# A two-bank tile for the first product of a state-exchange MoE kernel, with a new hand order for its first batch and a moved read in its last

## The chip, the cores and the metric

The kernel runs on one core of one Trainium2 chip. The metric is the device time of one execution in microseconds (us). Of the kernel before, three runs took 654.80, 655.16 and 655.46 us; their median, 655.16 us, is the time before. TensorE is called PE here, its weight loads PEld, VectorE DVE, ScalarE ACT, GpSimd POOL and SyncE SP, as in the profile.

## The reference

An attention between tokens and a small state, in both directions, feeds a two-layer feed-forward part with a piecewise quadratic in between:

```python
# x [8, 8, 512, 64], state [8, 8, 32, 64]  (batch, head, rows, 64)
scores = scale * x @ state.T            # softmax over 32 states
xread  = softmax(scores) @ state
scores2 = scale * state @ x.T           # softmax over 512 tokens
sread  = softmax(scores2) @ x
rows = concat([xread, sread], axis=2)   # -> [8 * 544, 512], heads side by side
h = rows @ w_in                         # [4352, 2048]
g = where(h >= 1, h, where(h <= -1, 0, (h + 1)**2 / 4))
out = g @ w_out                         # [4352, 512]
```

## The kernel before, in words

**Batches.** The eight batches of 512 token rows are worked one after the other, and the 256 `sread` rows of all batches together at the end as a ninth (`b == B`). For a token batch `xread @ w_in` is never formed from `xread`: the state is multiplied into `w_in` first (`sw`, a chunk of 256 columns at a time, one group of matmuls on 64x32 pieces of the array), and the normalised weights `ath`/`atl` are multiplied with that.

**Precision.** Each fp32 operand of a large product is split in two (`..h` a rounded high part, made by a copy on ACT; `..l` the rest, made by a subtraction on DVE), and each product is three matmuls: high x high, high x low, low x high (L473 to L475 for the first product, L529 to L531 for the second).

**A step.** Per batch there are eight steps `j`, each 256 columns wide. The first product (`product(0)` and `product(1)`, six matmuls each) goes to two PSUM tiles of one bank, tag `h`, two buffers. Then ACT takes `relu(0)`, `relu(1)` (L478) and `square` (L481), DVE `bound(0)`, `bound(1)` (L484, which reads the product in PSUM again), ACT `high` (L493, `gh`) and DVE `low` (L498, `gl`). The second product (`g2`, eight groups of three matmuls) of step `j` is issued after the first product of step `j + 1`, into four `acc` tiles of a bank each. PSUM has eight banks: four `acc`, two `h`, and one two-bank tile `mm` that scores, transposed weights and `sw` share. The tag `h` also holds `sr`, the read of the tokens by the state (`read2`, L323), in steps `j == 0` of later batches, and the two banks of the `sw` pair (chunks 5 and 6) in steps `j == 4`.

**Later batches** (L789 on) are written as a plain loop. The framework puts each engine's instructions in order from that program, by its own estimate of when each is ready, program order deciding between ready ones; a tile's buffer is given to the next user when all instructions that touch it are done. In the step `j == 0`, the loop issues the first product, the whole second product of the batch before, the `sr` read and its scaling (`scale2`, L331, DVE), four chunks of `sw` in two pairs that borrow the four `acc` banks, and, if there is a next batch, that batch's scores. After them come the splits of the chunks (L434 on ACT, L435 on DVE).

**The first batch** is different, since the weights have to be brought in: `w_in` and `w_out` arrive as eight chunks each of 1 MB in a wide format, and each takes two conversions (`high` L583 on ACT, `low` L575 on ACT or L570 on DVE), a join on DVE (L591) and, for `w_out`, a split (L598 on ACT, L602 on DVE). All of this is woven between the attention of batches 0 and 1 and the eight steps of batch 0. The weaving is a list, `ORDER` (L20): each word is the number of an operation and the engine that runs it (S, P, A, D). `Plan` (L37) computes begin times from the costs that the operations are given, sorts by them, emits in that order, and fills planned gaps of PE between the first scores and the first second product with `warm` matmuls (L170). Inside this stage the framework reorders nothing. `w_in` chunks are staged in two buffers (`raw`), so the DMA of each waits for the join of the chunk two before.

PE's order in the first batch of the kernel before (`p` is a first product half, with two numbers before the split by attention half; `g2.half.j`): warm, sc0, sw0, sw1, four half products of j=0, e2p0, p0(1), sw2, p1(1), g2.0.0, sr0, p0(2), sw3, p1(2), g2.1.0, sc1, p0(3), g2.0.1, p1(3), g2.0.2, sw4, g2.1.1, rt0, p0(4), sw5, p1(4), ... and a ninth `sw`, chunk 0 of batch 1, at the end.

Of the kernel before, what the change touches and what calls it, by code (L numbers as in the profile page):

```python
# [8 lines left out]
F32 = mybir.dt.float32  # L9
# [100 lines left out]
def state_exchange_moe(  # L110
# [42 lines left out]
    def ps_h(name):  # L153
        return ps.tile([P, 512], F32, tag="h", bufs=2, name=name)
# [42 lines left out]
    class Attention:  # L197
# [60 lines left out]
        def inv1(self, q):  # L258
            _, _, s = self.parts(q)
            nc.vector.tensor_scalar_add(s, s, 1e-9)  # L260
            nc.vector.reciprocal(out=s, in_=s)
# [113 lines left out]

    sw_of = {}

    def sw_product(b, c, n):

        pt = ps_mm(f"sw{b}_{c}")  # L380
        for i in range(n):
            for pr in range(NPR):
                for hh in range(2):
                    rows = slice(hh * 64, hh * 64 + 64)
                    nc.tensor.matmul(  # L385
                        pt[pr * NS:(pr + 1) * NS, hh, i * CI:(i + 1) * CI],
                        lhsT=sb[rows, b, pr], rhs=w32[c + i][rows, pr], start=True, stop=True,
                    )
        w = n * CI
        wh, wl = (  # L390
            v[:, :2 * w].rearrange("p (q f) -> p q f", q=2) for v in split_tiles(f"sw{b}_{c}")
        )
        sw_of[b, c] = pt[:, :, :w], wh, wl
        for i in range(n):
            cols = slice(i * CI, (i + 1) * CI)
            chunk[b, c + i] = wh[:, :, cols], wl[:, :, cols]

    def sw_high(b, c):
        pt, wh, _ = sw_of[b, c]
        nc.scalar.copy(out=wh, in_=pt)  # L400

    def sw_low(b, c):
        pt, wh, wl = sw_of[b, c]
        nc.vector.tensor_tensor(out=wl, in0=pt, in1=wh.bitcast(F32), op=ALU.subtract)

    def sw_make(b, c, n):
        sw_product(b, c, n)
        sw_high(b, c)
        sw_low(b, c)

    def sw_pair(pieces, banks, whole=None):
# [20 lines left out]
        def split():  # L432
            for h, lo, pt in parts:
                nc.scalar.copy(out=h, in_=pt)  # L434
                nc.vector.tensor_tensor(out=lo, in0=pt, in1=h.bitcast(F32), op=ALU.subtract)  # L435
# [13 lines left out]
    class Hidden:  # L449


        def __init__(self, b, j):
            self.b, self.j = b, j
            self.u = work.tile([P, 2, S], F32, tag="u", bufs=1, name=f"u{b}_{j}")
            self.hs = []

        def product(self, i, ks=None):
# [19 lines left out]
        def relu(self, i):  # L477
            nc.scalar.activation(out=self.u[:, i], in_=self.hs[i], func=AF.Relu, scale=0.5, bias=half)  # L478
# [4 lines left out]
        def bound(self, i):  # L483
            nc.vector.scalar_tensor_tensor(  # L484
                out=self.u[:, i], in0=self.u[:, i], scalar=1.0, in1=self.hs[i],
                op0=ALU.min, op1=ALU.max,
            )
# [118 lines left out]
    plan = Plan({"raw": 2, "mm": 1, "tmp": 2, "u": 1, "h": 2, "g": 2, "w": 2, "e2": 1, "xt": 1, "xn": 1})  # L606
# [278 lines left out]
```

## Time and profile before

| | |
|---|---|
| median of three runs | 655.16 us (654.80 to 655.46) |
| the profiled execution | 655.44 us, of which 653.6 us are its span |
| PE busy in the span | 643.5 us, 98% |
| ACT, DVE busy | 363.3 us (56%), 339.9 us (52%) |
| granted TensorE clock, mean | 0.999 |
| HBM traffic | 34.08 MB read, 8.91 MB written |

The span runs from the first to the last instruction; the rest of the time lies around it. A matmul's own duration includes its way through the array, so PE's rate is read from starts: matmuls of 512 columns follow each other every 0.227 us. Most of the run is the loop over batches 1 to 7, each 72.5 us long.

### The profile page before, as it was taken

The page shows a single profiled execution, that of the slowest core. Times are in us where ns is not written, and L with a number is a line of the kernel's source. Part 1 is how long each engine was busy: PE and PEld are TensorE (multiplying, and loading weights), DVE is VectorE, ACT ScalarE, POOL GpSimd, SP SyncE. Part 2 cuts the span into 40 slices and gives each one's busy share as a digit, 9 for nine tenths or more (in the row PEclk, how much of TensorE's full clock was granted, in tenths as well). Part 3 has the DMA queues.
Part 4 walks back from the last instruction along what each step waited for, and adds up shares of the span by engine and source line. Part 5 has one row for each costly group of instructions (what it writes and reads, how often), then busy time and mean ns, then how long its engine had stood idle before and what let it go on. Part 6 is the DMA issues. An engine that isn't in the chain of part 4 may idle for free.

```text
span 653.6 us, 10359 instructions
## 1 busy us (share of the span) xinstructions
PE 643.5 (98%) x4438; PEld 519.8 (80%) x4438; DVE 339.9 (52%) x511; ACT 363.3 (56%) x485; POOL 0.8 (0%) x7
## 2 busy tenths in 40 slices
PE   8899999999999999999999999999999999999997
PEld 6677787878787887878787887878787878788895
DVE  5998967533483338443574339343664335334431
ACT  4999856544565446554564456444664455444632
POOL 0000000000000000000000000000000000000000
PEclk9999999999999999999999999999999999999999
DMA  8996005000310004000500004000300010000101
GB/s 336 413 378 258 0 1 195 0 2 1 147 48 1 0 20 175 1 2 1 192 2 1 0 34 163 0 1 1 129 1 1 0 67 0 2 1 1 64 1 33
DMA packets 11085, 43.64 MB, mean 67 GB/s; under 512 B 1312, under 2 KB 1440, under 8 KB 7968
## 3 DMA queue, kind: packets, MB, share of 16 engines
q1 hardware_dynamic: 6096, 34.28, 13.4%
q10 hardware_dynamic: 4944, 8.72, 3.6%
q8 instruction: 34, 0.56, 0.3%
q14 instruction: 11, 0.09, 0.0%
HBM read 34.08 MB, written 8.91 MB: 66 GB/s over the span
## 4 chain that ended last, share of the span: by engine, by line
PE 96%; DVE 2%; ACT 0%; issue 0%; DMA 0%; POOL 0%; SPq 0%; POOLq 0%
PE acc L529 19%; PE acc L531 19%; PE acc L530 19%; PE h L473 10%; PE h L474 10%; PE h L475 10%; PE sw L421 4%; PE sr L323 1%; PE sc L225 1%; PE e2p L305 1%; PE warmed L170 1%; PE sw L385 1%; DVE w L591 1%; DMA out_dram<-o 0%; DVE z L232 0%
## 5 line engine op out<-in xcount | busy, mean ns | idle before, releaser
L529 PE MATMUL acc<-wo,gh 128*128 128x512 f32 x544 | 214.0, 393 | 0.0
L531 PE MATMUL acc<-wo,gl 128*128 128x512 f32 x544 | 211.9, 390 | 0.0
L530 PE MATMUL acc<-wo,gh 128*128 128x512 f32 x544 | 211.9, 390 | 0.0
L478 ACT ACTIVATE u<-h,half 128x512 f32<-128x512 f32 x136 | 93.1, 689 | 179.8 <-PE h L475 170.4
L484 DVE SCALAR_TENSOR_TENSOR u<-u,h 128x512 f32<-128x512 f32 x136 | 87.3, 682 | 196.5 <-ACT u L481 196.2
L529 PEld LDWEIGHTS acc<-wo,gh 128*128 128x128 f32 x544 | 102.1, 188 | 24.4 <-issue 3.3
L531 PEld LDWEIGHTS acc<-wo,gl 128*128 128x128 f32 x544 | 102.1, 188 | 21.7
L530 PEld LDWEIGHTS acc<-wo,gh 128*128 128x128 f32 x544 | 102.2, 188 | 20.5
L498 DVE TENSOR_TENSOR gl<-u,gh 128x1024 fp32r<-128x1024 f32 x68 | 83.3, 1225 | 58.1 <-ACT gh L493 58.1
L493 ACT CAST gh<-u 128x1024 fp32r<-128x1024 f32 x68 | 71.4, 1051 | 63.5 <-DVE u L484 63.5
L481 ACT ACTIVATE u<-u 128x1024 f32<-128x1024 f32 x68 | 72.1, 1061 | 1.8
L421 PE MATMUL sw<-w,sb 64*32 64x256 f32 x880 | 27.0, 379 | 0.0
L544 ACT COPY o<-acc 128x512 f32<-128x512 f32 x33 | 19.0, 583 | 12.1 <-PE acc L531 12.1
L473 PE MATMUL h<-ath,sw_1h 128*128 128x512 f32 x60 | 24.4, 407 | 0.9 <-DVE u L484 0.9
L474 PE MATMUL h<-ath,sw_1l 128*128 128x512 f32 x60 | 23.5, 392 | 0.2 <-DVE sw_1l L435 0.2
L473 PE MATMUL h<-ath,sw_5h 128*128 128x512 f32 x60 | 23.6, 393 | 0.0
L473 PE MATMUL h<-ath,sw_3h 128*128 128x512 f32 x60 | 23.5, 391 | 0.0
L474 PE MATMUL h<-ath,sw_5l 128*128 128x512 f32 x60 | 23.4, 390 | 0.0
L475 PE MATMUL h<-atl,sw_5h 128*128 128x512 f32 x60 | 23.4, 389 | 0.0
L475 PE MATMUL h<-atl,sw_1h 128*128 128x512 f32 x60 | 23.4, 389 | 0.0
L475 PE MATMUL h<-atl,sw_3h 128*128 128x512 f32 x60 | 23.4, 389 | 0.0
L474 PE MATMUL h<-ath,sw_3l 128*128 128x512 f32 x60 | 23.3, 389 | 0.0
(184 smaller groups left out, 733.2 us busy)
## 6 DMA issues: line engine op xcount, KB each, us to landing
xt<-in_xt_dram SPq DMA_DIRECT2D x16, 512.0 KB, 5.0
raw_i<-in_moe_w_in_dram SPq DMA_DIRECT2D x8, 1024.0 KB, 6.0
raw_o<-in_moe_w_out_dram SPq DMA_DIRECT2D x8, 1024.0 KB, 11.4
xn<-in_x_dram SPq DMA_DIRECT2D x8, 1024.0 KB, 6.0
out_dram<-o ACTq DMA_DIRECT2D x32, 256.0 KB, 2.0
sb<-in_state_dram SPq DMA_DIRECT2D x1, 448.0 KB, 12.8
out_dram<-o SPq DMA_DIRECT2D x4, 64.0 KB, 1.7
out_dram<-o ACTq DMA_DIRECT2D x4, 64.0 KB, 2.0
```

The lines of the kernel that those rows point to most:

```text
L421: nc.tensor.matmul(banks[hh][pr * NS:(pr + 1) * NS, cols], lhsT=sb[rows, b, pr], rhs=w32[c][rows, pr], start=True, stop=True,)
L473: nc.tensor.matmul(o, lhsT=wh[:, k, sl], rhs=ah[:, k], start=first, stop=False)
L474: nc.tensor.matmul(o, lhsT=wl[:, k, sl], rhs=ah[:, k], start=False, stop=False)
L475: nc.tensor.matmul(o, lhsT=wh[:, k, sl], rhs=al[:, k], start=False, stop=last)
L478: nc.scalar.activation(out=self.u[:, i], in_=self.hs[i], func=AF.Relu, scale=0.5, bias=half)
L481: nc.scalar.activation(out=self.u, in_=self.u, func=AF.Square)
L484: nc.vector.scalar_tensor_tensor(out=self.u[:, i], in0=self.u[:, i], scalar=1.0, in1=self.hs[i], op0=ALU.min, op1=ALU.max,)
L493: nc.scalar.copy(out=gh, in_=self.u)
L498: nc.vector.tensor_tensor(out=gl, in0=self.u, in1=gh.bitcast(F32), op=ALU.subtract)
L529: nc.tensor.matmul(a, lhsT=lh, rhs=oh, start=f == 0, stop=False)
L530: nc.tensor.matmul(a, lhsT=lh, rhs=ol, start=False, stop=False)
L531: nc.tensor.matmul(a, lhsT=ll, rhs=oh, start=False, stop=f == NF - 1)
```

## The change

Four things change together.

- **One tile for the first product.** The tag `h` becomes one buffer of two banks in place of two buffers of one. `product(i)` writes bank `i` of it. `sr` takes the whole tile (using a corner of bank 0), and the `sw` pair of step `j == 4` takes both its banks.
- **First batch, fewer and larger operations.** `relu` and `bound` run once over both banks (128x1024); the two `inv1` of an attention become one pair of small instructions over both halves (in the loop's `first` as well). The chunks of `sw` are made as (0), (1), (2), (3, 4), (5, 6), (7 and batch 1's 0): three alone and three pairs, where there were nine alone. The loop over later batches goes on calling `relu(i)` and `bound(i)` bank by bank.
- **First batch, another order.** `ORDER` is replaced, and some costs in the plan are other numbers. PE's order becomes: warm, sc0, sw0, two half products of j=0, sw1, the other two, sw2, p0(1), p1(1), e2p0, g2.0.0, sr0, p0(2), sw3+4, p1(2), g2.1.0, sc1, p0(3), g2.0.1, p1(3), g2.0.2, g2.1.1, p0(4), sw5+6, p1(4), g2.1.2, g2.0.3, p0(5), rt0, p1(5), sw7+, g2.1.3, p0(6), g2.0.4, p1(6), g2.1.4, g2.0.5, p0(7), e2p1, p1(7), g2.0.6, g2.1.5, g2.1.6. The DMA order on SP becomes xt0, i0, i1, o0, o2, i2, o1, i4, xn0, i3, sb, xt1, i6, o7, o3, o6, i5, o4, i7, o5, xn1 (`i` and `o` are chunks of `w_in` and `w_out`; before: o0, o1, i2, i3, xt1, o2, xn0, o3, sb, o4, i4, i5, o7, o5, xn1, i6, i7, o6). DVE's order up to the first second product is: turns and maxima of batch 0, less, sum, inv1, w0, norm, back, norm, swl0, atl, back, w1, atl, top2, low i2, swl1, w2, top2, bound(0), join o0, swl2, gl(0), wol 0.
- **Last batch (b = 7), step j == 0.** `read2` is issued behind the four `sw` chunks instead of ahead of them, and `scale2` behind their splits.

```diff
     def ps_h(name):
-        return ps.tile([P, 512], F32, tag="h", bufs=2, name=name)
+        return ps.tile([P, 2, 512], F32, tag="h", bufs=1, name=name)
...
-        def inv1(self, q):
-            _, _, s = self.parts(q)
-            nc.vector.tensor_scalar_add(s, s, 1e-9)
-            nc.vector.reciprocal(out=s, in_=s)
+        def inv1(self):
+            nc.vector.tensor_scalar_add(self.s1, self.s1, 1e-9)
+            nc.vector.reciprocal(out=self.s1, in_=self.s1)
...
-            sr = ps_h(f"sr{b}") if b else ps_mm(f"sr{b}")[:, 0]
+            sr = (ps_h if b else ps_mm)(f"sr{b}")[:, 0]
...
         def first(self):
-            for f in (self.top1, self.less1, self.exp1, self.sum1, self.inv1, self.norm1):
+            for f in (self.top1, self.less1, self.exp1, self.sum1):
                 for q in range(2):
                     f(q)
+            self.inv1()
+            for q in range(2):
+                self.norm1(q)
...
         def product(self, i, ks=None):
...
-            if not ks or 0 in ks:
-                self.hs.append(ps_h(f"h{b}_{j}_{i}"))
-            hp = self.hs[i]
+            if i == 0 and (not ks or 0 in ks):
+                self.h = ps_h(f"h{b}_{j}")
+            hp = self.h[:, i]
...
-        def relu(self, i):
-            nc.scalar.activation(out=self.u[:, i], in_=self.hs[i], func=AF.Relu, scale=0.5, bias=half)
+        def relu(self, i=slice(None)):
+            nc.scalar.activation(out=self.u[:, i], in_=self.h[:, i], func=AF.Relu, scale=0.5, bias=half)
...
-        def bound(self, i):
+        def bound(self, i=slice(None)):
             nc.vector.scalar_tensor_tensor(
-                out=self.u[:, i], in0=self.u[:, i], scalar=1.0, in1=self.hs[i],
-                op0=ALU.min, op1=ALU.max,
+                out=self.u[:, i], in0=self.u[:, i], scalar=1.0, in1=self.h[:, i], op0=ALU.min, op1=ALU.max
             )
...
-        for i in range(2):
-            op(("relu", i) + k, "ACT", 0.58, lambda i=i: hid[k].relu(i), [("p", i) + k], ends=[("h", i) + k],
-               take=[("u", ("u",) + k)] if i == 0 else [])
-        op(("square",) + k, "ACT", 0.97, lambda: hid[k].square(), [("relu", 0) + k, ("relu", 1) + k])
-        for i in range(2):
-            op(("bound", i) + k, "DVE", 0.6, lambda i=i: hid[k].bound(i), [("square",) + k], ends=[("h", i) + k])
+        op(("relu",) + k, "ACT", 0.98, lambda: hid[k].relu(), [("p", i) + k for i in range(2)], ends=[("h",) + k],
+           take=[("u", ("u",) + k)])
+        op(("square",) + k, "ACT", 0.97, lambda: hid[k].square(), [("relu",) + k])
+        op(("bound",) + k, "DVE", 1.14, lambda: hid[k].bound(), [("square",) + k], ends=[("h",) + k])
...
+    def sw_ops(*pieces):
+        n, k = len(pieces), pieces[0]
+        unit.update((p, k) for p in pieces)
+
+        def product():
+            pt = ps_mm("sw{}_{}".format(*k))
+            unit["split", k] = sw_pair(pieces, [pt[:, hh] for hh in range(2)], pt)
...
+    more = {0: [(0, 2)], 1: [(0, 3), (0, 4)], 3: [(0, 5), (0, 6)], 5: [(0, 7), (1, 0)]}
     for j in range(NJ):
         g1_ops(0, j)
         hidden_ops(0, j)
-        if j + 1 < NC:
-            sw_ops(0, j + 1, 1)
+        if j in more:
+            sw_ops(*more[j])
...
         if j == 0:
-            atts[b].read2()
-            atts[b].scale2()
+            if nxt:
+                atts[b].read2()
+                atts[b].scale2()
             halves = [
                 sw_pair([(b, c), (b, c + 1)], [ps_acc(f"sw{b}_{c}_{hh}") for hh in range(2)]) for c in (1, 3)
             ]
...
+            else:
+                atts[b].read2()
             for split in halves:
                 split()
             if nxt:
                 nxt.second()
+            else:
+                atts[b].scale2()
...
-            own = [ps_h(f"sw{b}_5_{hh}") for hh in range(2)]
-            split = sw_pair([(b, 5), (b, 6)], own)
+            own = ps_h(f"sw{b}_5")
+            split = sw_pair([(b, 5), (b, 6)], [own[:, hh] for hh in range(2)])
```

More of the change, by code (lines that the diff above doesn't have):

```diff
@@ L374, in state_exchange_moe @@
     chunk = {}
[L376 to L409, printed above, removed]
     def sw_pair(pieces, banks, whole=None):
@@ L430, in sw_pair, with split @@
             parts = [(wh[:, hh, :n], wl[:, hh, :n], banks[hh][:, :n]) for hh in range(2)]
-        def split():
+        def split(part=None):
             for h, lo, pt in parts:
-                nc.scalar.copy(out=h, in_=pt)
-                nc.vector.tensor_tensor(out=lo, in0=pt, in1=h.bitcast(F32), op=ALU.subtract)
+                if part != 1:
+                    nc.scalar.copy(out=h, in_=pt)
+                if part != 0:
+                    nc.vector.tensor_tensor(out=lo, in0=pt, in1=h.bitcast(F32), op=ALU.subtract)
         return split
@@ L602, in part_low @@
         nc.vector.tensor_tensor(out=wl, in0=parts[c], in1=wh.bitcast(F32), op=ALU.subtract)
[L606 removed]
+    plan = Plan({"raw": 2, "mm": 1, "tmp": 2, "u": 1, "h": 1, "g": 2, "w": 2, "e2": 1, "xt": 1, "xn": 1})
     op = plan.op
@@ L658, in att_ops1 @@
             op(("sum1",) + k, "DVE", 0.62, m("sum1", q), [("exp1",) + k])
-            op(("inv1",) + k, "DVE", 0.4, m("inv1", q), [("sum1",) + k])
-            op(("norm1",) + k, "DVE", 0.62, m("norm1", q), [("inv1",) + k])
+        op(("inv1", b), "DVE", 0.42, m("inv1"), [("sum1", b, q) for q in range(2)])
         for q in range(2):
             k = (b, q)
+            op(("norm1",) + k, "DVE", 0.62, m("norm1", q), [("inv1", b)])
             take = [("tmp", ("zt", b))] if q == 0 else []
@@ L702, in product @@
         hid[b, j].product(i, ks)
-    def sw_ops(b, c, n):
-        tensor(("sw", b, c), 0.35 + 0.35 * n, lambda: sw_product(b, c, n), [("w", c + i) for i in range(n)],
-               take=[("mm", ("sw", b, c)), ("w", ("wc", b, c))])
-        op(("swh", b, c), "ACT", 0.5 * n, lambda: sw_high(b, c), [("sw", b, c)], ends=[("sw", b, c)])
-        op(("swl", b, c), "DVE", 0.6 * n, lambda: sw_low(b, c), [("swh", b, c)], ends=[("sw", b, c)])
-    def g1_ops(b, j):
-        if j == 0:
-            for q in range(2):
-                for i in range(2):
-                    need = [(x, b, j) for x in ("swh", "swl")] + [(x, b, q) for x in ("ath", "atl")]
-                    tensor(("p", i, b, j) if q else ("p0", i), 0.72, lambda i=i, q=q: product(i, b, j, [q]), need,
-                           take=[] if q else [("h", ("h", i, b, j))], ends=[("wc", b, j)])
-            return
-        for i in range(2):
-            need = [(x, b, j) for x in ("swh", "swl")] + [(x, b, q) for x in ("ath", "atl") for q in range(2)]
-            tensor(("p", i, b, j), 1.4, lambda i=i: product(i, b, j), need, take=[("h", ("h", i, b, j))],
-                   ends=[("wc", b, j)])
+    unit = {}
@@ new lines, in sw_ops @@
+    def sw_ops(*pieces):
[4 more added lines that the diff above has]
+            unit["split", k] = sw_pair(pieces, [pt[:, hh] for hh in range(2)], pt)
+        tensor(("sw",) + k, 0.36 + 0.43 * n, product, [("w", c) for _, c in pieces],
+               take=[("mm", ("sw",) + k), ("w", ("wc",) + k)])
+        op(("swh",) + k, "ACT", 0.5 * n, lambda: unit["split", k](0), [("sw",) + k], ends=[("sw",) + k])
+        op(("swl",) + k, "DVE", 0.6 * n, lambda: unit["split", k](1), [("swh",) + k], ends=[("sw",) + k])
@@ new lines, in g1_ops @@
+    def g1_ops(b, j):
+        u = unit[b, j]
+        for i in range(2):
+            for q in range(2) if j == 0 else [None]:
+                need = [(x,) + u for x in ("swh", "swl")]
+                need += [(x, b, k) for x in ("ath", "atl") for k in range(2) if q in (k, None)]
+                first = i == 0 and not q
+                tensor(("p0", i) if q == 0 else ("p", i, b, j), 1.37 if q is None else 0.7,
+                       lambda i=i, q=q: product(i, b, j, None if q is None else [q]), need,
+                       take=[("h", ("h", b, j))] if first else [], ends=[("wc",) + u])
@@ L723, in g2_ops @@
     def g2_ops(b, j, half):
         k = (b, j)
-        tensor(("g2", half) + k, 2.75, lambda: g2(b, j, (4 * half, 4 * half + 4)), [("gh",) + k, ("gl",) + k, ("wol", j), ("sc done", 0)],
+        tensor(("g2", half) + k, 2.74, lambda: g2(b, j, (4 * half, 4 * half + 4)), [("gh",) + k, ("gl",) + k, ("wol", j), ("sc done", 0)],
                ends=[("g",) + k])
@@ L755, in state_exchange_moe @@
     op(("sc done", 0), "ACT", 0, lambda: None, [("exp2", 0, 0), ("exp2", 0, 1)])
[L756 removed]
+    sw_ops((0, 0))
+    sw_ops((0, 1))
     between = {
[L758 removed]
+        0: lambda: tensor(("e2p", 0), 0.92, lambda: atts[0].turn2(), [("exp2", 0, 0), ("exp2", 0, 1)],
                           take=[("mm", ("e2p", 0))]),
[L760 removed]
+        1: lambda: tensor(("sr", 0), 1.23, lambda: atts[0].read2(), [("kept", 0), ("dma", "xn", 0)],
                           take=[("mm", ("sr", 0))], ends=[("e2", 0), ("xn", 0)]),
[L762 removed]
+        2: lambda: tensor(("sc", 1), 1.22, lambda: att_start(1), [("dma", "sb", 1), ("dma", "xt", 1)],
                           take=[("mm", ("sc", 1))], ends=[("xt", 1)]),
[L764 to L765 removed]
+        3: lambda: tensor(("rt", 0), 0.15, lambda: atts[0].keep2(), [("rs", 0)], take=[("mm", ("rt", 0))]),
+        4: lambda: tensor(("e2p", 1), 0.92, lambda: atts[1].turn2(), [("exp2", 1, 0), ("exp2", 1, 1)],
                           take=[("mm", ("e2p", 1))]),
     }
+    more = {0: [(0, 2)], 1: [(0, 3), (0, 4)], 3: [(0, 5), (0, 6)], 5: [(0, 7), (1, 0)]}
     for j in range(NJ):
```

11 lines of the change are left out of this document (1 added, 10 removed), and 25 rows, old and new, of the table ORDER.

## The prediction

> **What bounds the kernel now.** I read the page's totals first, then the busy time by stretches (us; engine and busy time, instructions in brackets), then the timeline at the places that the change touches.
>
> ```profile
> span 653.6 us, 10359 instructions
> PE 643.5 (98%) x4438; PEld 519.8 (80%) x4438; DVE 339.9 (52%) x511; ACT 363.3 (56%) x485; POOL 0.8 (0%) x7
> ...
> PE 96%; DVE 2%; ACT 0%; issue 0%; DMA 0%; POOL 0%; SPq 0%; POOLq 0%
> ```
>
> ```profile
> 0.00:30.00 30.00, 24.59 (x207) 19.66 (x208) 22.05 (x42) 20.52 (x27) 0.83 (x7) 1.00 0.92 370
> 30.00:93.00 63.00, 63.00 (x427) 47.51 (x426) 58.16 (x79) 54.12 (x68) 0.00 (x0) 1.00 0.45 183
> 93.00:165.50 72.50, 72.50 (x507) 58.41 (x506) 35.73 (x57) 38.58 (x53) 0.00 (x0) 1.00 0.12 44
> ...
> 536.00:542.00 6.00, 5.85 (x140) 4.22 (x140) 3.08 (x6) 3.33 (x6) 0.00 (x0) 1.00 0.24 90
> ```
>
> PE (the first number behind the comma) has no idle time from 30 us on, and the chain of waits is PE for 96%. DVE and ACT are half idle in the loop. So only three things can move the end: the moment at which PE becomes dense (about 30 us), the amount of PE work behind it, and holes that the change opens or closes. One hole stands in the last batch, at 536 to 542. The clock column (1.00) leaves nothing to win.
>
> **The start of the dense stretch.** In the first 30 us the second product waits for the splits that DVE makes:
>
> ```profile
> 28.21 1.22 DVE L498 TENSOR_TENSOR gl<-u,gh 128x1024 fp32r<-128x1024 f32 x1
> ...
> 29.87 0.40 PE L529 MATMUL acc<-wo,gh 128*128 128x512 f32 x1
> 30.10 0.39 PE L530 MATMUL acc<-wo,gh 128*128 128x512 f32 x1
> ...
> 19.00:30.00 11.00, 9.80 (x73) 7.62 (x66) 10.57 (x18) 10.71 (x17) 0.00 (x0) 1.00 1.00 417
> ```
>
> DVE is busy 10.57 of the 11 us up to there, ACT 10.71: the start is the sum of DVE's work in front of the last operand of the first `g2`, which the new order can only shuffle. By the two lists of operations, the same work stands in front of it, except that one pair of `inv1` instructions is gone and the split of chunk 2 has come forward:
>
> ```profile
> 11.88 0.17 DVE L260 TENSOR_SCALAR s<-s 128x16 f32<-128x16 f32 x1
> ...
> 12.26 0.63 DVE L247 TENSOR_TENSOR z<-z,m 128x512 f32<-128x512 f32 x1
> ```
>
> The pair takes 12.26 - 11.88 = 0.38 us. A split of 128x512 takes half of the 1.28 that two in a row need (540.16, quoted under the last batch), 0.64. So +0.26. Against it stands the idle time of DVE that a better order could close, 11.00 - 10.57 = 0.43. Bounds: -0.3 (most of it closed, the split hidden) and +0.5 (0.26, and a new gap as long). I take 0, since the two nearly cancel, and PE has the same work in front of it in both orders (`sw` 0 to 2, both first products, `e2p0`).
>
> **PE's work behind it.** What one chunk of `sw` takes PE, alone and among four:
>
> ```profile
> 49.33 0.39 PE L531 MATMUL acc<-wo,gl 128*128 128x512 f32 x1
> 49.65 0.66 PE L385 MATMUL sw<-w,sb 64*32 64x256 f32 x16
> 50.24 0.50 PE L529 MATMUL acc<-wo,gh 128*128 128x512 f32 x1
> 50.57 0.39 PE L530 MATMUL acc<-wo,gh 128*128 128x512 f32 x1
> ...
> 208.97 0.39 PE L531 MATMUL acc<-wo,gl 128*128 128x512 f32 x1
> 209.29 1.96 PE L421 MATMUL sw<-w,sb 64*32 64x256 f32 x64
> ...
> 211.52 0.40 PE L530 MATMUL acc<-wo,gh 128*128 128x512 f32 x1
> ```
>
> Matmuls of 512 columns follow each other every 0.227 us (0.23 from 29.87 to 30.10). One chunk alone: 50.57 - 49.33 less two such spaces = 0.79. Four: 211.52 - 208.97 - 0.45 = 2.10. So a further chunk in a group costs (2.10 - 0.79) / 3 = 0.44, and the entry and exit that each group pays once 0.35. Three pairs save 3 x 0.35 = **1.05 us** of PE time, all of it behind the start (chunks 3 to 7 and the next batch's 0).
>
> **The one tile: what is queued behind the new wait.** `product(0)` of step j + 1 now needs `bound` over both banks, where it needed `bound(0)`; behind it on PE waits all later work. From the loop, a step's own chain:
>
> ```profile
> 167.87 0.39 PE L475 MATMUL h<-atl,sw_7h 128*128 128x512 f32 x1
> ...
> 168.29 0.69 ACT L478 ACTIVATE u<-h,half 128x512 f32<-128x512 f32 x1 [0.67 <-PE h L475]
> ...
> 170.11 1.28 DVE L484 SCALAR_TENSOR_TENSOR u<-u,h 128x512 f32<-128x512 f32 x2 [4.48 <-ACT u L481]
> ...
> 25.10 0.99 ACT L309 COPY e<-e2p 128x1024 f32<-128x1024 f32 x1
> ```
>
> From the start of the last matmul to both bounds' end: 171.39 - 167.87 = 3.52. No row has a 128x1024 `relu` from PSUM. The nearest is the ACT copy of that size from PSUM, 0.99; the upper bound is two halves, 1.38. I take 1.1, nearer the copy. For `bound` on 128x1024 I take the 1.22 of `gl`, with the 1.28 of two halves as the upper end. The merged chain is 3.52 + (1.1 - 0.69) - 0.06 = 3.87, between 3.76 and 4.21. In the first batch PE must have that much other work before it comes back to `h`. By the new order the shortest such spells are between steps 2 and 3 (half a second product, then the scores) and between 5 and 6 (a pair, half a second product). Half a second product is 12 x 0.227 = 2.73; scores about 1.1 (64 matmuls of a chunk group take 1.96, the 16 twice as wide ones of the scores about half); a pair 0.79 + 0.44 = 1.23. With the last matmul's own 0.23 that is 4.1 and 4.2: some 0.2 to 0.3 us of cover. Elsewhere two halves, 5.5 us, lie between. In the loop 24 matmuls, 5.45 us, lie between steps, so relu and bound by halves are covered there with 1.9 us to spare (5.45 - 3.52). Stalls: from 0 to 2 x 0.8, if a weight conversion of about 1.1 us just started stands in front of `relu` or `square` at both thin places. I take 0.1.
>
> On the other side ACT and DVE are relieved: each merged relu saves 0.28 of 1.38 on ACT at my value. Since PE sets the end from 30 us on, I book nothing for that; without PE as the cover it would be worth about 2 us over eight steps on ACT, 0.5 on DVE. The same holds for `inv1` in the loop (0.38 a batch).
>
> The Trainium skill, Perfetto Trace Analysis, "Optimizing Scalar/DVE Operations", says that grouping helps where the engine is saturated, and that breaking instructions up helps where it isn't and holds up another engine. Here both hold in turn: ACT is saturated up to 30 us, and in the thin spells the merged relu would start later than the first half relu did. By the rule for the second case the sum would lose what the chain grew by at each thin spell, at most 2 x 0.35; by the rows above the cover of 0.2 to 0.3 us takes most of it.
>
> **Moved DMAs.** SP issues 22 loads as before. `o2` takes `o1`'s place in front of `i2`, so the same bytes are ahead of it; `i2` still waits for the join of chunk 0.
>
> ```profile
> 14.65 2.96 SPq L563 DMA_DIRECT2D raw_i<-in_moe_w_in_dram  x2
> ...
> raw_i<-in_moe_w_in_dram SPq DMA_DIRECT2D x1, 1024.0 KB, 4.7
> ...
> 21.14 1.15 ACT L583 ACTIVATE raw_i<-raw_i 128x1024 f32<-128x1024 f32 x1
> ```
>
> It lands 4.7 us after 14.65 and is first read at 21.14: 1.8 us of cover. Of the moved ones `i3` is the tightest. At 417 GB/s a megabyte takes 2.5 us, and behind `i2` come `o1`, `i4`, `xn0`, `i3`: landed at 19.35 + 4 x 2.5 = 29.4, read by DVE after the split of `o0` and the conversions of `i4`, not before 31. Nothing booked; lateness would go straight into step 2.
>
> **The last batch.** Without a next batch's scores, PE reaches the first product of step 1 before its chunk is split:
>
> ```profile
> 536.12 1.10 PE L323 MATMUL sr<-xn,e 128*32 128x64 f32 x64
> ...
> 537.16 1.96 PE L421 MATMUL sw<-w,sb 64*32 64x256 f32 x64
> 537.29 0.29 DVE L331 TENSOR_TENSOR rs<-sr,r 128x128 f32<-128x128 f32 x1 [0.99 <-PE sr L323]
> ...
> 538.96 1.29 DVE L435 TENSOR_TENSOR sw_1l<-sw,sw_1h 128x512 fp32r<-128x512 f32 x2 [1.37 <-ACT sw_1h L434]
> 539.04 0.51 PE L473 MATMUL h<-ath,sw_1h 128*128 128x512 f32 x1
> ...
> 539.70 0.50 PE L474 MATMUL h<-ath,sw_1l 128*128 128x512 f32 x1 [0.15 <-DVE sw_1l L435]
> ...
> 540.16 1.28 DVE L435 TENSOR_TENSOR sw_3l<-sw,sw_3h 128x512 fp32r<-128x512 f32 x2
> ```
>
> The second matmul follows the first after 0.66 us, where 0.33 is usual after such a group (50.24 to 50.57): 0.33 lost. With `sr` behind the chunks, its 1.04 us (537.16 - 536.12) fill that hole: **-0.33**. The chunks then start at 536.12, and the second pair needs the last of the four `acc` banks copied out by ACT; if that is late it costs part of a copy, at most 0.59 (row below). I book nothing, since the first pair runs for 0.9 us meanwhile.
>
> But `sr` now holds the one `h` tile until `scale2`, which the program puts behind the four subtractions. These end at 541.44 now and would end 1.04 earlier, 540.40; with `scale2` the tile is free at 540.7, while PE is through with `sr` at 539.0 (536.12 + 1.88 + 1.04, the old spacings). In that hole of 1.7 us three or four groups of three matmuls of batch 7's own second product fit (its operands were split before the chunks): each needs one `acc` bank, and these come free one by one at 538.6, 539.2, 539.8, 540.4. The trace shows that the framework moves ready work forward, on ACT:
>
> ```profile
> 533.51 0.59 ACT L544 COPY o<-acc 128x512 f32<-128x512 f32 x1 [0.46 <-PE acc L531]
> 534.00 1.05 ACT L493 CAST gh<-u 128x1024 fp32r<-128x1024 f32 x1
> ```
>
> `gh` stands ahead of that copy in the program. If it does the same on PE, the hole is filled.
>
> **Sum**, against the profiled execution (span 653.6 and 1.84 around it, 655.44, which is 0.28 over the median): start 0, pairs -1.05, stalls +0.1, last batch -0.33: -1.28. Span 652.3, that execution 654.2, median 655.16 - 1.28 = **653.9 us**. Own range from the bounds: -0.3 - 1.05 - 0.33 = -1.7 (653.5), and +0.5 - 1.05 + 0.7 (one thin place missed by most of 0.8) - 0.33 = -0.2 (655.0).
>
> **Rivals.**
> *A, the tile held in the last batch.* PE keeps program order and waits for `scale2`: 1.7 us of hole, and the 0.33 of today goes. -1.28 + 1.7 = +0.4: 655.6. For it: program order decides on PE everywhere that I looked. Against: the ACT rows above; in the trace PE never had ready work behind a held tile, so it doesn't decide.
> *B, the tile stalls the first batch*, so that the pairs bring nothing. The two thin spells miss by 0.5 each, a conversion's half: +1.0 in place of 0.1 leaves 654.8. For it: the thin cover, in a stretch where DVE is busy 58.16 of 63 us. Against: the old order, with as full engines, has no hole.
> The Trainium skill, Perfetto Trace Analysis, "Optimizing Tensor Performance", asks that independent matmul groups rotate through PSUM banks, so that the evacuation of one runs under the next; the new tile leaves no free bank to rotate to. The loop's trace agrees that 3.5 us of evacuation lie under 5.5 us of other matmuls, which is why I give it weight in the thin spells alone.
> *C, slower.* In step 4 the `sw` pair of the loop sits in the `h` tile. Its subtractions must both end before the next first product, which before needed only the first.
>
> ```profile
> 211.41 1.28 DVE L435 TENSOR_TENSOR sw_5l<-sw,sw_5h 128x512 fp32r<-128x512 f32 x2
> 212.61 1.21 DVE L435 TENSOR_TENSOR sw_7l<-sw,sw_7h 128x1024 fp32r<-128x1024 f32 x1
> ...
> 213.38 0.40 PE L473 MATMUL h<-ath,sw_5h 128*128 128x512 f32 x1
> ```
>
> They end at 212.69, PE comes at 213.38. If DVE's order puts the 1.21 us one between them, they end at 213.9, and PE stalls 0.5 in each of seven batches: +3.5 - 1.3 = +2.2: 657.4. It decides from 0.7 us of lateness on. Against it: program order has them in front.
>
> **Chances.** Forecast 0.52, A 0.16, B 0.18, C 0.08, and 0.06 for more gain (the start comes 0.3 and another 0.4 of DVE's idle time earlier, 653.2). This measurement can tell about 0.2%, 1.3 us, from no change: faster begins below 653.85. That bound cuts the forecast in two, with 0.32 of its 0.52 below, since its lower bound is the better founded; with the larger gain and a little of B that is 0.40 faster, 0.48 within, 0.12 slower (C, and A with B and a late load together). The range for 8 in 10 reaches from somewhat below the larger gain to just over A: 652.9 to 655.9.
>
> **What would show it.** Batch 1's first product starts here now:
>
> ```profile
> 92.87 0.39 PE L473 MATMUL h<-ath,sw_0h 128*128 128x512 f32 x1
> ```
>
> It should start near 91.9; at 92.9 B is right. PE idle ahead of L473 naming `bound` between 40 and 80 us is B. A group of 32 matmuls of `sw` three times before 80 us is the pairs. In the last batch, second-product matmuls between `sr` and the first product of step 1 show the filled hole, idle PE there is A. Loop batches of 72.5 us exclude C.

## The result, and the profile after

The changed kernel takes **679.36 us** (median of six runs, 679.18 to 679.61), the kernel before on the same chip 655.04 us (six runs, 654.80 to 655.46). The ratio is **1.0371, 95% interval 1.0357 to 1.0384**: 24.3 us slower. Forecast were 653.9 us and a range up to 655.9, so the prediction was wrong in sign and in size.

The page's totals, and the chain of work that ended last, by engine:

```profile
span 677.3 us, 10333 instructions
...
PE 663.8 (98%) x4438; PEld 513.9 (76%) x4438; DVE 340.6 (50%) x484; ACT 360.2 (53%) x474; POOL 0.8 (0%) x7
...
PE 77%; DVE 13%; ACT 7%; issue 2%; DMA 0%; POOL 0%; ACTq 0%; DVEq 0%; POOLq 0%
```

PE runs as many matmuls as before (4438) and is still busy for 98% of the span. That share says nothing of the loss, because waiting matmuls look longer. The chain says more: it was PE for 96%, and now goes over DVE and ACT for 20%. Busy time by stretches (start to end, length, then PE, PEld, DVE, ACT, POOL busy with their instructions):

```profile
30.00:91.50 61.50, 61.37 (x425) 47.73 (x424) 56.70 (x68) 52.05 (x57) 0.00 (x0) 1.00 0.48 193
91.50:167.15 75.65, 75.32 (x507) 57.48 (x506) 34.61 (x53) 38.13 (x53) 0.00 (x0) 1.00 0.12 43
```

The first batch is over at 91.48 us, 1.39 earlier than before (92.87). A batch of the loop, with the same 507 matmuls and the same granted clock (1.00), takes 75.65 us where it took 72.50. That stage has no instruction more or less on PE. From the first products of the batches: batch 7 starts at 545.57, before at 527.87, which is +17.70 = -1.39 + 6 x 3.18; the last batch and the ninth take another 6.0 (677.3 - 545.57 against 653.6 - 527.87). So **everything that was lost was lost where the program text hardly changed**. What PE's weight loads waited for (us in total, times, longest):

```profile
PEld h L440 <- ACT u L445: 16.6, 58, 0.4
PEld acc L497 <- DVE gl L464: 8.3, 23, 0.5
PEld h L440 <- DVE u L451: 8.0, 18, 1.0
...
PEld sw L387 <- DVE u L451: 4.6, 7, 0.8
```

The first line has no counterpart before: the first product waits, 58 times, for a `relu` (L445; L478 in the kernel before). No `relu` makes anything that the first product reads. What it touches is the other bank of the tile. One step of the loop (second batch, j = 4) before shows ACT's `relu(0)` and `relu(1)` and DVE's `gl`. From `relu(0)` to the start of `gl` ACT and DVE run nothing else, and in step j = 7, which holds no `sw` group, the chain is as long, 6.87 us:

```profile
204.64 0.69 ACT L478 ACTIVATE u<-h,half 128x512 f32<-128x512 f32 x1 [2.56 <-PE h L475]
...
206.00 0.69 ACT L478 ACTIVATE u<-h,half 128x512 f32<-128x512 f32 x1 [0.67 <-PE h L475]
...
210.27 1.23 DVE L498 TENSOR_TENSOR gl<-u,gh 128x1024 fp32r<-128x1024 f32 x1 [1.17 <-ACT gh L493]
```

And step j = 7 of the second batch after, called the quiet step below, from the timelines of ACT, DVE, PE and PE's weight loads:

```profile
234.95 1.22 DVE L464 TENSOR_TENSOR gl<-u,gh 128x1024 fp32r<-128x1024 f32 x1 [1.17 <-ACT gh L459]
235.48 0.39 PE L442 MATMUL h<-atl,sw_7h 128*128 128x512 f32 x1
...
236.23 0.19 PEld L497 LDWEIGHTS acc<-wo,gl 128*128 128x128 f32 x1 [0.33 <-DVE gl L464]
...
236.27 0.69 ACT L445 ACTIVATE u<-h,half 128x512 f32<-128x512 f32 x1 [1.35 <-DVE gl L464]
...
237.01 0.19 PEld L440 LDWEIGHTS h<-ath,sw_7h 128*128 128x128 f32 x1 [0.26 <-ACT u L445]
...
238.28 0.39 PE L442 MATMUL h<-atl,sw_7h 128*128 128x512 f32 x1
...
238.70 0.69 ACT L445 ACTIVATE u<-h,half 128x512 f32<-128x512 f32 x1 [1.75 <-PE h L442]
...
240.52 1.29 DVE L451 SCALAR_TENSOR_TENSOR u<-u,h 128x512 f32<-128x512 f32 x2 [4.35 <-ACT u L448]
...
242.97 1.23 DVE L464 TENSOR_TENSOR gl<-u,gh 128x1024 fp32r<-128x1024 f32 x1 [1.17 <-ACT gh L459]
```

The last matmul of `product(0)` starts at 235.48, then PE does five second-product matmuls, and only when `relu(0)` has read bank 0 does `product(1)` start writing bank 1, at 237.0. Before, `relu(1)` followed `relu(0)` after 1.36 us (the six matmuls between them); now it follows after 2.43. By these 1.07 us everything behind it in the step is later (from `relu(0)` to the end of `gl` 7.93 us now, 236.27 to 242.97 + 1.23, where it was 6.86, 204.64 to 210.27 + 1.23). So `gl` of the step before, and with it the one buffer of `u`, isn't ready when PE and ACT come for it (236.23 and 236.27). The quiet step costs 8.48 us instead of 8.16. In the step with the attention's second softmax (j = 1) it is worse, since the late `relu(1)` there falls behind other work of ACT. Before:

```profile
180.45 0.69 ACT L478 ACTIVATE u<-h,half 128x512 f32<-128x512 f32 x1 [0.67 <-PE h L475]
...
181.43 0.69 ACT L294 ACTIVATE e<-sc,nm 128x512 f32<-128x512 f32 x1 [0.28 <-DVE nm L291]
```

After, in the batch before that one:

```profile
105.36 0.69 ACT L445 ACTIVATE u<-h,half 128x512 f32<-128x512 f32 x1 [1.20 <-PE h L442]
...
107.70 0.69 ACT L292 ACTIVATE e<-sc,nm 128x512 f32<-128x512 f32 x1 [1.65 <-DVE nm L289]
...
109.04 0.69 ACT L445 ACTIVATE u<-h,half 128x512 f32<-128x512 f32 x1
```

`relu(1)` comes 3.68 us behind `relu(0)`, since the two exponentials of the second softmax came first, and the chain that ended last runs there over ACT and DVE. Step by step (distance between the first products of successive steps, second batch of the loop):

| step | 0 | 1 | 2 | 3 | 4 and 5 | 6 | 7 | batch |
|---|---|---|---|---|---|---|---|---|
| before | 12.03 | 8.45 | 9.07 | 8.16 | 18.47 | 8.16 | 8.16 | 72.50 |
| after | 12.19 | 8.90 | 9.66 | 8.33 | 19.64 | 8.49 | 8.48 | 75.69 |

Every step loses something; 4 and 5 together, where the `sw` pair sits in the tile, lose most.

### The profile page after: what moved, and what is told of

Its sections match the earlier page's. It is cut to its first block, busy times and chain, and to the rows that moved or that the text cites. A ratio compares the mean times of both kernels' runs of the same rounds, so it can differ in the third digit from the quotient of the medians.

```text
span 677.3 us, 10333 instructions
## 1 busy us (share of the span) xinstructions
PE 663.8 (98%) x4438; PEld 513.9 (76%) x4438; DVE 340.6 (50%) x484; ACT 360.2 (53%) x474; POOL 0.8 (0%) x7
## 4 chain that ended last, share of the span: by engine, by line
PE 77%; DVE 13%; ACT 7%; issue 2%; DMA 0%; POOL 0%; ACTq 0%; DVEq 0%; POOLq 0%
PE acc L497 15%; PE acc L495 15%; PE acc L496 14%; PE h L440 10%; PE h L441 8%; PE h L442 8%; PE sw L387 4%; DVE u L451 3%; ACT u L448 2%; ACT u L445 2%; DVE gl L464 2%; DVE sw_1l L403 1%; DVE z L231 1%; ACT e L292 1%; DVE sw_3l L403 1%
## 5 line engine op out<-in xcount | busy, mean ns | idle before, releaser
L451 DVE SCALAR_TENSOR_TENSOR u<-u,h 128x512 f32<-128x512 f32 (+1 forms) x128 | 86.9, 718 | 217.2 <-ACT u L448 216.9
L445 ACT ACTIVATE u<-h,half 128x512 f32<-128x512 f32 (+1 forms) x128 | 91.6, 716 | 191.3 <-PE h L442 159.3
L387 PE MATMUL sw<-w,sb 64*32 64x256 f32 x1024 | 36.4, 380 | 3.6 <-DVE w L557 2.4
L387 PEld LDWEIGHTS sw<-w,sb 64*32 64x32 f32 x1024 | 18.6, 106 | 16.7 <-DVE u L451 4.6
L440 PE MATMUL h<-ath,sw_1h 128*128 128x512 f32 x60 | 26.5, 441 | 1.3 <-DVE u L451 0.5
L440 PE MATMUL h<-ath,sw_5h 128*128 128x512 f32 x64 | 27.0, 421 | 0.1
L440 PE MATMUL h<-ath,sw_3h 128*128 128x512 f32 x64 | 26.8, 418 | 0.0
L442 PE MATMUL h<-atl,sw_5h 128*128 128x512 f32 x64 | 25.1, 393 | 0.0
L441 PE MATMUL h<-ath,sw_3l 128*128 128x512 f32 x64 | 25.1, 392 | 0.0
L440 PE MATMUL h<-ath,sw_7h 128*128 128x512 f32 x60 | 24.9, 416 | 0.1
```

Of the source, the lines that this page charges most:

```text
L387: nc.tensor.matmul(banks[hh][pr * NS:(pr + 1) * NS, cols], lhsT=sb[rows, b, pr], rhs=w32[c][rows, pr], start=True, stop=True,)
L440: nc.tensor.matmul(o, lhsT=wh[:, k, sl], rhs=ah[:, k], start=first, stop=False)
L441: nc.tensor.matmul(o, lhsT=wl[:, k, sl], rhs=ah[:, k], start=False, stop=False)
L442: nc.tensor.matmul(o, lhsT=wh[:, k, sl], rhs=al[:, k], start=False, stop=last)
L445: nc.scalar.activation(out=self.u[:, i], in_=self.h[:, i], func=AF.Relu, scale=0.5, bias=half)
L451: nc.vector.scalar_tensor_tensor(out=self.u[:, i], in0=self.u[:, i], scalar=1.0, in1=self.h[:, i], op0=ALU.min, op1=ALU.max)
```

## The experiments

Two theories stood against each other at first. **Theory 1**: the framework orders engines by tile, so a write to one bank waits for a read of the other bank of the same tile; two tiles of a bank each don't have that. **Theory 2**, in several forms below: the loss comes from the tile having a single buffer, or from the new first batch or the moved read behind it. Each run was compared with runs of the kernel before on the same chip.

**The tile alone (e7).** The kernel before; only the loop's `h` became a two-bank tile.

```diff
-                self.hs.append(ps_h(f"h{b}_{j}_{i}"))
+                if b:
+                    if i == 0:
+                        two = ps_h2(f"h{b}_{j}")
+                        self.hs = [two[:, 0], two[:, 1]]
+                else:
+                    self.hs.append(ps_h(f"h{b}_{j}_{i}"))
...
-            own = [ps_h(f"sw{b}_5_{hh}") for hh in range(2)]
+            own = ps_h2(f"sw{b}_5")
+            split = sw_pair([(b, 5), (b, 6)], [own[:, hh] for hh in range(2)])
```

> The kernel before with nothing of the change but the one two-bank tile for the loop's first products, the reads of the state and the step-4 pair; the first batch keeps two tiles of one bank and its old order. Theory 1 (the tile in the loop is the whole loss): loop batches of 75.6 us and 678.5 to 681.5. Theory 2 (a part of the loss comes from the rest of the change, the order of the first batch or the moved read): below 672.

Measured: 680.17 us (679.94 to 681.00), ratio 1.0385 (1.0370 to 1.0399). Its first product's wait for `relu`, and a batch of its loop:

```profile
PEld h L483 <- ACT u L488: 17.0, 58, 0.5
```

```profile
168.28:244.00 75.72, 75.33 (x507) 57.48 (x505) 35.79 (x56) 38.18 (x54) 0.00 (x0) 1.00 0.12 43
```

The same wait, the same 58 times, the same batch. The tile in the loop, 25.0 us here, is the whole loss; the first batch and the moved read have no part in it.

**The same banks as two tiles (e3).** The changed kernel, whose first batch keeps the two-bank tile; behind it the tile's pool is closed, and one of two one-bank buffers takes its place. By the programs' lists of allocations the loop's first product lies in PSUM banks 6 and 7 in the kernel before, in the changed one, in e7 and in e3 alike, so the chip sees the same addresses, written and read by the same engines.

```diff
+    hp[0].__exit__(None, None, None)
+    hpool[0] = ctx.enter_context(tc.tile_pool(name="hp1", bufs=2, space=PSUM))
     loaded["xt", 2] = load_xt(2)
     for i, (b, j) in enumerate(steps):
...
+                if i == 0:
+                    self.hs = []
+                self.hs.append(ps_h1(f"h{b}_{j}_{i}"))
```

> The changed kernel with the loop's first product, its sr and its paired chunks of step 4 back in two one-bank tiles (the first batch keeps the two-bank tile, whose banks are handed over between the first batch and the loop); the program order of the loop is as changed. Theories 1 and 2 both: batches of 72.5 us, 653.3 us. If something else of the change slows the loop (the merged inv1, chunk 0 of batch 1 made in a pair), it stays near 679.

Measured: 654.18 us (eleven runs, 653.71 to 654.83), ratio **0.9985 (0.9976 to 0.9995)**. That is 0.9 us above the 653.3 expected, which counted on batch 1 starting 1.4 us earlier, as in the one trace of the changed kernel. Only 0.82 us of that are a shorter first batch (62.18 us in place of 63.00); the start itself spreads by 0.9 us from run to run, as shown further down. A batch of its loop:

```profile
91.79:164.29 72.50, 72.50 (x507) 58.44 (x505) 35.16 (x54) 38.59 (x53) 0.00 (x0) 1.00 0.12 44
```

All of the loss is gone. So it isn't the chip: PE writes bank 7 while ACT reads bank 6 at no cost in time. The order is put in by the program. The list of PE's instructions shows it, with the semaphore that each waits for, at the first matmul of `product(1)` in step j = 7 of the second batch, changed kernel ahead of the one before:

```
L440 MATMUL h_7_1996<-ath_903,sw_7h 128x512 [waits Activation_49]
L473 MATMUL h_7_1_2068<-ath_947,sw_7h 128x512 [waits DVE_49]
```

The changed program waits for ACT there (the `relu` of the other bank), the one before for DVE (the `bound` that last read this bank in the step before). The Trainium skill, PSUM — Partial Sum Buffer, "PSUM bank collisions raise a hardware error", gives as its rule that engines be kept apart by semaphores "by bank × quadrant (by bank is the simple version)". Two tiles of a bank each follow that rule, and the traces agree that nothing more is lost; the two-bank tile is kept apart more coarsely than the rule asks, at 25 us (e7).

**Both products first (e1).** The changed kernel, but in the loop `product(1)` stands ahead of `relu(0)` in the program, so that it has nothing to wait for.

```diff
         for i in range(2):
             hid.product(i)
+        for i in range(2):
             hid.relu(i)
```

> The changed kernel with one thing else: in the loop over later batches the program issues both halves of a first product before the first relu (product, product, relu, relu in place of product, relu, product, relu). The single two-bank tile stays. Theory 1 (the framework orders the second half behind the relu of the first half because both touch one tile, and so pulls the first product apart): PE runs all 12 matmuls of a first product in a row again, the loop's batches go from 75.7 back to 72.5 us, and the time is 655.0 - 1.4 (batch 1 started 1.4 us earlier in the changed kernel) - 0.3 = 653.3 us. Theory 2 (the single buffer: the next first product and the paired chunks of step 4 wait for both bounds): order of issue changes nothing in that, 676 to 680 us.

Measured: 663.16 us (663.05 to 663.37), ratio 1.0122 (1.0108 to 1.0136). 16.2 of the 24.3 us come back, a batch takes 73.8; the rest stays, which theory 1, as put here, didn't foresee. Its step 4 shows why:

```profile
206.09 1.27 ACT L445 ACTIVATE u<-h,half 128x512 f32<-128x512 f32 x2 [3.35 <-PE h L442]
...
211.03 0.59 ACT L401 CAST sw_5h<-sw 128x512 fp32r<-128x512 f32 x1
...
212.08 0.68 DVE L403 TENSOR_TENSOR sw_5l<-sw,sw_5h 128x512 fp32r<-128x512 f32 x1
...
212.80 0.59 ACT L401 CAST sw_5h<-sw 128x512 fp32r<-128x512 f32 x1 [1.18 <-DVE sw_5l L403]
...
213.41 0.69 DVE L403 TENSOR_TENSOR sw_5l<-sw,sw_5h 128x512 fp32r<-128x512 f32 x1 [0.65 <-ACT sw_5h L401]
```

The tile works in the other direction too: `relu(0)` now waits for all twelve matmuls, and both `relu` run back to back behind them. And reads take turns: ACT's copy of the second bank waits for DVE's subtraction from the first (1.18 us idle), and DVE's second waits for that copy. Before, the two copies ran back to back and the two subtractions behind (211.41):

```profile
210.48 1.08 ACT L434 CAST sw_5h<-sw 128x512 fp32r<-128x512 f32 x2 [0.24 <-PE sw L421]
```

The wait is in the program: the one semaphore on ACT's second copy is DVE's, counted to the first subtraction, where in the kernel before it is PE's, counted to the copy's own matmuls. The copies also write the halves of one SBUF tile, `sw_5h`, which the subtractions read; but the kernel before has that tile too, without such a wait, so the PSUM tile makes the difference. So it isn't only a write that is ordered against a read, but a read on ACT against a read on DVE as well. That is a wider rule than the one I started from; the next three runs test it.

**One pass in the loop (e2).** e1, with `relu` and `bound` over both banks at once, as the first batch has them.

```diff
-        for i in range(2):
-            hid.relu(i)
+        hid.relu()
         hid.square()
-        for i in range(2):
-            hid.bound(i)
+        hid.bound()
```

> The changed kernel, and in the loop too both halves of a first product come first and then relu and bound in one pass over both banks. Theory 1: 653.3 us as well, since the evacuation chain grows by about 0.4 us to 3.9 and 5.4 us of other matmuls lie over it; where step 4 leaves only 3.6 us before the paired chunks, up to 0.3 us a batch are lost, 2 us in all, so 653 to 655.5. Theory 2: a longer hold of the single tile makes it worse than the changed kernel, 680 us or more.

Measured: 659.05 us (658.94 to 659.59), ratio 1.0061 (1.0048 to 1.0074), a batch 73.04: between the two theories' numbers. Step 1 is at its old length (8.45), since the one `relu` is through before the exponentials; steps 4 and 5 together take 19.04 us where they took 18.47, which is all that this batch still loses.

**The pair in one pass (e5 and e6).** e1 and e2, with the step-4 pair of chunks read by one copy and one subtraction.

```diff
-            split = sw_pair([(b, 5), (b, 6)], [own[:, hh] for hh in range(2)])
+            split = sw_pair([(b, 5), (b, 6)], [own[:, hh] for hh in range(2)], own)
```

> The kernel of e1 with the step-4 pair of chunks in the `h` tile split in one pass (one ACT copy and one DVE subtraction over both banks, where e1 has two of each). Theory 1 (any touch of one bank of the tile waits for the last touch of the other bank, so ACT and DVE read in turns): the turns copy, subtract, copy, subtract took 211.03 to 214.10 in e1; one copy and one subtraction over both banks take about 1.0 and 1.2, so the next first product comes 0.6 to 0.9 us earlier in each of 7 batches: 657 to 659, step 4 at 10.3 to 10.4. Theory 2 (what is left in e1 comes from the single buffer of the tile, which is free only when its last reader ends, however the reading is cut): the last subtraction ends no earlier, 662.5 to 664.

> The kernel of e2 (relu and bound in one pass in the loop) with the step-4 pair of chunks split in one pass too: nothing in the loop touches the two-bank tile in halves on ACT or DVE. Theory 1 (per-tile order is the whole loss): e2's loop batch of 73.04 us loses its last 0.54, so 654.0 to 655.5. Theory 2 (the single buffer, not the turns): 658.5 to 659.5, loop batch 73.0.

Measured: e5 660.47 us (660.35 to 661.07), ratio 1.0084 (1.0070 to 1.0097), 2.7 below e1; e6 656.99 us (656.26 to 657.38), ratio 1.0027 (1.0017 to 1.0038), 2.1 below e2. (e1 and e2 ran on another chip, where the kernel before took 655.27 us; here it took 655.15.) Both miss both theories' numbers. The turns are gone in e5. Its step 4:

```profile
206.45 1.27 ACT L445 ACTIVATE u<-h,half 128x512 f32<-128x512 f32 x2 [3.35 <-PE h L442]
...
209.75 2.40 PE L387 MATMUL sw<-w,sb 64*32 64x256 f32 x64
...
212.44 1.22 DVE L403 TENSOR_TENSOR sw_5l<-sw,sw_5h 128x1024 fp32r<-128x1024 f32 x1
```

Counted from `relu(0)`, the pair is split after 7.21 us (206.45 to 213.66), in e1 after 8.01 (206.09 to 214.10): the turns cost 0.80, as expected, but the batch gains only half of it (73.79 to 73.41). The other half is not to be had, because PE's own `sw` group, which the wait for `bound(1)` stretches to 2.40 us (1.96 in the kernel before), is then what ends last. The expectation had taken the turns for the only thing late there. In e6 a batch is 72.75, 0.25 over the old one. Its `sw` group of step 4:

```profile
208.48 2.21 PE L387 MATMUL sw<-w,sb 64*32 64x256 f32 x64
```

and that of e3:

```profile
208.21 1.96 PE L392 MATMUL sw<-w,sb 64*32 64x256 f32 x64
```

In e3 both `bound`s have ended at 208.01, ahead of the pair. In e6 `relu` begins behind all twelve matmuls, the chain is later for it, and the one `bound` ends at 208.65 (207.43 + 1.22): the group's first matmul, which waits for DVE in the program, begins at 208.48 and is still alone at 208.7, so that the group of 64 takes 2.21 us instead of 1.96. The tile is free as a whole or not at all, which is what theory 2 said of the one buffer, though this is a small part of what it was asked to explain. In six full batches it is 1.5 of the 2.5 us by which e6's span is longer than e3's (654.9 and 652.4); the last batch and the ninth lose the other 1.0 (126.6 from batch 7's start to the end, against 125.6).

The loop batches in a row: one tile as changed 75.65; both products first 73.79; `relu` and `bound` in one pass as well 73.04; the pair as well 72.75; two tiles 72.50.

**The first batch alone (e9).** e3 with the read of the last batch back at its old place.

```diff
-            if nxt:
-                atts[b].read2()
-                atts[b].scale2()
+            atts[b].read2()
+            atts[b].scale2()
```

> The kernel of e3 with the last batch's read of the state back at its old place: of the change only the first batch is left (one tile there, one pass, pairs, the new order). Theory 1 (the pairs and one-pass relu and bound shorten the first batch by 0.82 us, the interval that e3's trace shows from its first second-product matmul to batch 1): 0.6 to 1.0 us below the kernel before, 654.2 to 654.5 on this chip if before stands at 655.1; e3's stretch from batch 7's first product to the end, 125.6 us, goes back to 125.7. Theory 2 (the moved read carries most of e3's gain): within 0.3 us of the kernel before.

Measured: 654.32 us (eleven runs, 653.91 to 654.93), ratio 0.9986 (0.9977 to 0.9995): 0.9 us (0.14%) faster, as expected from the trace.

**The moved read alone (e4), and its tile (e8).** e4 is the kernel before with `read2` and `scale2` behind the chunks in the last batch; e8 is e3 with that read in the `mm` tile.

```diff
-            sr = ps_h1(f"sr{b}") if b else ps_mm(f"sr{b}")[:, 0]
+            sr = ps_h1(f"sr{b}") if 0 < b < B - 1 else ps_mm(f"sr{b}")[:, 0]
```

> The kernel before with only the last batch's read behind its four chunks and the scaling behind their splits. With two one-bank tiles nothing holds the next first product, so the 0.33 us hole ahead of its second matmul closes: the distance from the start of the read or the chunks to the second matmul of step 1 falls from 3.58 us (536.12 to 539.70) to 3.25, and the time by 0.3 us, below what a run can tell.

> The kernel of e3 (two tiles in the loop) with the last batch's read of the state in the `mm` tile instead of an `h` tile, so that the first product of step 1 needs no buffer that the scaling holds. Theory 1 (in e3 and e4 that buffer opens a gap of 0.35 us ahead of the second half of the first product, 539.22 to 539.58): the gap goes, 653.8 to 654.0, 0.2 to 0.4 below e3. Theory 2 (the `mm` tile is late itself, as the transpose after it takes the same tile): 654.2 or above.

Measured: e4 654.43 us in its one run, beside 655.27 before (654.39 to 655.83), which one run can't tell apart. Its trace closes the hole ahead of the second matmul as expected (3.25 us, 535.29 to 538.54), but opens a gap ahead of `product(1)`, because the read's buffer is held until the scaling ends. e3 has the same gap (last matmul of `product(0)`, first of `product(1)`):

```profile
539.22 0.40 PE L453 MATMUL h<-atl,sw_1h 128*128 128x512 f32 x1
...
539.58 0.50 PE L451 MATMUL h<-ath,sw_1h 128*128 128x512 f32 x1
```

and e8 hasn't: 0.36 us became 0.23 (539.65 to 539.88). From batch 7's first product to the end of the span the traces have 125.73 before, 125.83 in e9, 125.61 in e3 and 125.39 in e8. **e8 takes 653.93 us (eleven runs, 653.74 to 654.38), ratio 0.9981 (0.9972 to 0.9990)**, the shortest time of these kernels and as theory 1 had it. That it is better than e3, which ran on another chip, rests on the trace; the intervals overlap.

## Why the prediction was wrong

**The step that failed** is a sentence in the part on the one tile: "In the loop 24 matmuls, 5.45 us, lie between steps, so relu and bound by halves are covered there with 1.9 us to spare (5.45 - 3.52)." The arithmetic holds, but it was reckoned for a chain of 3.52 us in which the second half follows the first as the matmuls do, with all 24 matmuls behind it. That chain came from the kernel with two tiles. I asked who must wait for the *whole* tile at the end of a step, and not whether the two halves of it still run beside each other within a step. They don't: `relu(1)` follows `relu(0)` by 2.43 us instead of 1.36, five of the 24 matmuls move in between the halves of the first product, and e7 puts the price of that and its consequences at 25 us, where the sum had 0. The cover itself holds in the quiet step (the chain from the last matmul, 238.28, ends at 241.81, and PE comes back at 242.82). In two of the eight steps of a batch, j = 2 and j = 6, it no longer does, and the next first product waits for `bound`:

```profile
188.22 0.19 PEld L440 LDWEIGHTS h<-ath,sw_1h 128*128 128x128 f32 x1 [0.55 <-DVE u L451]
...
225.80 0.19 PEld L440 LDWEIGHTS h<-ath,sw_5h 128*128 128x128 f32 x1 [0.21 <-DVE u L451]
```

**Rival C** had a right place, and the order that it feared came. It looked at the step-4 pair in the tile, feared that DVE would put the 1.21 us subtraction between the two of the pair, and was put aside because "program order has them in front". That order was not kept: ACT's second copy of the pair has to wait for DVE's first subtraction, and the framework put `sw_7`, the group of chunk 7, in between, on ACT and on DVE. Step 4 of the changed kernel, second batch:

```profile
212.59 2.73 PE L387 MATMUL sw<-w,sb 64*32 64x256 f32 x64
...
215.61 0.68 DVE L403 TENSOR_TENSOR sw_5l<-sw,sw_5h 128x512 fp32r<-128x512 f32 x1
216.45 1.23 DVE L403 TENSOR_TENSOR sw_7l<-sw,sw_7h 128x1024 fp32r<-128x1024 f32 x1 [0.16 <-ACT sw_7h L401]
217.59 0.68 DVE L403 TENSOR_TENSOR sw_5l<-sw,sw_5h 128x512 fp32r<-128x512 f32 x1
...
218.60 0.39 PE L440 MATMUL h<-ath,sw_5h 128*128 128x512 f32 x1
```

But PE doesn't stand for it, as C had it: it does 14 second-product matmuls behind the group, where the kernel before does nine, and shows no wait at 218.60. What the step does lose is the wait of the `sw` group for `bound(1)`, 2.73 us in place of 1.96. And it was a part only: in the changed kernel steps 4 and 5 lose 1.17 of 3.19 us a batch. Its sign that "Loop batches of 72.5 us exclude C" worked: they were 75.65, and pointed to the loop at once.

**The rule on rotating banks** (the Trainium skill, Perfetto Trace Analysis, "Optimizing Tensor Performance") was given "weight in the thin spells alone". The runs show the reverse: no loss in the thin spells, and all of it in the loop, where I had taken the trace of two tiles for the trace of one.

**The rest of the sum held**, as e3 and e9 show. Forecast for it was -1.28; e3, the change without the tile in the loop, measured -1.09 (655.27 to 654.18; by its interval, between -1.6 and -0.3). Its terms:

- *The start*, 0: can't be told. The first second-product matmul is at 29.87 in the kernel before and at 28.99 in e4, whose first batch is the same program, so 0.9 us is the spread from run to run; after it is 29.30, within that.
- *The pairs*, -1.05, and *stalls*, +0.1. In the changed kernel a pair stands like this, with the limits of the first batch's dense stretch around it:

```profile
29.30 0.48 PE L495 MATMUL acc<-wo,gh 128*128 128x512 f32 x1
...
53.66 0.39 PE L442 MATMUL h<-atl,sw_3h 128*128 128x512 f32 x1
53.98 1.09 PE L387 MATMUL sw<-w,sb 64*32 64x256 f32 x32
...
55.34 0.40 PE L441 MATMUL h<-ath,sw_3l 128*128 128x512 f32 x1
...
91.48 0.39 PE L440 MATMUL h<-ath,sw_7h 128*128 128x512 f32 x1
```

  55.34 - 53.66 less two spaces is 1.23, the 0.79 + 0.44 of the forecast. The stretch is 62.18 us (29.30 to 91.48), before 63.00: -0.82 for -0.95. In its last 61.5 us PE idles 0.13 (61.37 of 61.50, above), the stall term of 0.1; 0.1 of the pairs' gain is not accounted for.
- *The two durations without a row*: `relu` and `bound` over 128x1024 were taken as 1.1 and 1.22, and measured 1.119 and 1.219. ACT and DVE groups of the first batch:

```profile
L445 ACT ACTIVATE u<-h,half 128x1024 f32<-128x1024 f32 x8 | 9.0, 1119 | 1.4 <-PE h L442 1.4
...
L451 DVE SCALAR_TENSOR_TENSOR u<-u,h 128x1024 f32<-128x1024 f32 x8 | 9.8, 1219 | 3.3 <-ACT u L448 3.1
```

- *Rival B*, stalls in the first batch, doesn't show: the stretch became shorter, and there `relu` and `bound` work on both banks at once, so there are no halves to be ordered.
- *The last batch*, -0.33, and *rival A*. The hole is filled by the framework, as hoped, with five second-product matmuls between the read and the first product; some 0.3 us of it stay, up to the end of the scaling, where A had 1.7:

```profile
555.98 1.10 PE L321 MATMUL sr<-xn,e 128*32 128x64 f32 x64
...
557.01 0.50 PE L495 MATMUL acc<-wo,gh 128*128 128x512 f32 x1
...
558.62 0.47 PE L440 MATMUL h<-ath,sw_1h 128*128 128x512 f32 x1 [0.18 <-DVE rs L329]
```

  The gain has to be read where the loop doesn't cover it: -0.34 in e8 (125.73 to 125.39) and -0.12 in e3, where the second half of the first product needs the buffer that the read still holds.

So the small terms were reckoned to a tenth of a microsecond, and the one assumption that carried 25 us had no row of its own in the profile before. With two tiles the trace cannot show how one would be ordered. That case belonged among the rivals, with a price from the rows.

## What to carry to other kernels

A PSUM tile is the unit by which this framework orders engines: before two buffers are merged into one, list every pair of instructions on different engines that today work on the two halves at the same time, and count each of them as one behind the other, reads included. Merge only where every reader and writer takes the whole tile in one pass (even then e6 lost 0.25 us a batch), and keep tiles of one bank wherever the work goes by halves; the same two banks can be one tile in one stage of a kernel and two in another. After a change, compare the stages whose text did not change first: here they held all of the loss.

## What the runs showed that I had not expected

- Two engines that only *read* different banks of one tile are put in turn: ACT's second copy idled 1.18 us for DVE's first subtraction (212.80 in e1).
- With a single tile, the framework took `product(1)` apart from `product(0)` and put second-product matmuls of the step before between them (235.48 and 237.01 above). This filled PE, but the wait it hid on PE made the chain on ACT and DVE 1.07 us longer, and that came back as other waits in each step.
- PE's busy share is 98% before and after, with a span of 653.6 and of 677.3: a matmul that waits inside a group is counted as a longer matmul (the `sw` group of step 4 shows 2.73 us for 1.96), so the share of the chain (PE 96% to 77%) was the first number to show the loss.
